# First keys loaded in two halves around the queries, first scores asked after half the keys, first hashes in the AV banks

## Chip, cores, metric

One core of a Trainium2 chip. The metric is the device time of the whole program in microseconds (us). The span of a profile is a little under the time of the same run (765.1 us against 766.81 us for the kernel before). With one core there is no second die to compare with, so "fast" here only says that a run lies within 1.5% of the fastest run of its kernel.

## The reference, cut

Hash attention over 4 batches, 8 heads, 768 tokens, 64 dimensions. A query sees the keys that share its 6-bit hash. The result feeds a dense mixture of 8 experts, which is most of the time and is not touched.

```python
q_bits = (np.einsum('bhsd,dk->bhsk', q, proj) > 0)      # k_bits likewise
mask = q_bucket[:, :, :, None] == k_bucket[:, :, None, :]
scores = np.where(mask, scale * np.matmul(q, k.transpose(0, 1, 3, 2)), -1e9)
attn = np.exp(scores - scores.max(-1, keepdims=True))
out = np.matmul(attn / (attn.sum(-1, keepdims=True) + 1e-09), v)
# [cut] then the experts: out += P[:, e:e+1] * (np.maximum(x @ w1[e], 0) @ w2[e])
```

## The kernel before

Heads are worked in groups of four. The mask is part of the matmul: six hash bits and one constant row are appended to the 64 dimensions (`KR` is 71 rows), with the key bits scaled by `BIG`. For every group, keys and queries are loaded, turned (transposed) on VectorE (DVE), hashed on TensorE (PE) and cast to f16. PE then makes scores for 24 units (4 heads x 6 key tiles), ScalarE (ACT) exponentiates each, PE multiplies with the values. I count these units from 0 through all groups, so unit 6 is the first of head 1, unit 24 the first of the second group, unit 30 of that group's head 1.

The first group goes through `at_once`. The second group is prepared between the first group's units; the hash bits of its heads 1 to 3 go out to DRAM and come back to other partitions (`put_bits`, `get_bits`).

```python
def fetch(n, what, eng=nc.gpsimd):          # [cut] addresses
    for name, src in (("k", k), ("q", q)):
        if name in what:
            pin(eng.dma_start(out=t, in_=src[...]))            # 768 KB, 6144 B per partition
    if "v" in what:
        for m in range(M4):                                    # 4 transfers to 32 partitions each
            pin(eng.dma_start(out=t[R * m:R * (m + 1)], in_=vsrc[m]))

def at_once():                              # the first group
    for name in "kq":
        d["pr" + name] = sps.tile([P, 2, 512], F32, tag="s", name="pr0")   # a bank of the scores' pool
        turn_qk(name, 0)                                       # DVE, then a GpSimd cast
        place(name, 0, 0, nc.scalar.copy)                      # ACT cast of head 0
        hash_twice(name, 0)                                    # PE, 4 matmuls into 4 x 32 partitions
        turn_qk(name, 1)
        # [cut] more casts on ACT, hash_twice(name, 1), warm-up matmuls, stacks of heads 2 and 3
    # [cut] key bits for all heads, moved to head 0; query bits of head 0; query bits for all heads
    place("q", 1, 1, nc.vector.tensor_copy)
    move("k", 1)                                               # DVE bit copies of head 1
    move("q", 1)
    # [cut] stack("q", 3), get_bits, cast_v() on GpSimd

def prepare(n):                             # later groups, [cut] turns, hash, stacks
    put_bits()                                                 # SP: bits to DRAM
    for h in range(1 if n < 3 else 0, 2):
        get_bits("k", h); get_bits("q", h)                     # SP: and back
    # [cut] stacks and bits of heads 2 and 3
    if n == 1:
        fetch(2, "kq")                                         # GpSimd's queue: 1.5 MB
        load_w(0, 1, pin=True, half=0)                         # and expert weights

fetch(0, "kq", nc.sync)
fetch(0, "v", nc.sync)
fetch(1, "kq", nc.sync)
# [cut] offsets, warm_up(16), the first group, then the loop over the units
```

The softmax here doesn't subtract the row's maximum and nothing guards it: scores larger than these inputs give would overflow.

## Time and profile before

| | before |
|---|---|
| time, median of 3 runs | 766.77 us (766.58 to 767.16) |
| DVE starts to turn the queries | 8.94 us |
| first exponential, unit 6, unit 17 | 14.27, 18.90, 28.91 us |
| next group's four transposes start | 18.21 us |
| first PE turn of finished heads | 27.97 us |

The prediction below shows the page's header, the chain and the DVE timeline. This is the queue of SyncE (SP) of before in order of time (start, length of the issue, engine, line, operation, out<-in):

```profile
25.90 0.53 SPq L422 DMA_DIRECT2D ds<-bt  x1
...
33.40 0.27 SPq L425 DMA_DIRECT2D ks<-ds  x1
33.72 0.30 SPq L425 DMA_DIRECT2D qs<-ds  x1
```

The second group's bits leave for DRAM (`ds`) at 25.90 and can be read back only when that write has landed, at 33.40: 7.5 us for 96 KB.

### The profile page before, as it was taken

Reading aid. Unit: us, or ns where it says so; the run is one execution under the profiler, and the core shown is the slowest. Engines: PE = TensorE matmul, PEld = TensorE weight load, DVE = VectorE, ACT = ScalarE, POOL = GpSimd, SP = SyncE. Lnnn points to the kernel's source line nnn. Section 1 sums busy time; section 2 is a strip of 40 time slices with the busy share of each in tenths; the row PEclk is TensorE's granted clock in tenths of the full one; section 3 lists DMA queues with packets and bytes.
Section 4 is the critical chain, followed back from the end, with each engine's and each line's share of the span. In section 5 each row is a group of like instructions: output and inputs, shape, how many; then the busy total and the mean of one; then the engine's idle time right before and its main releaser. Section 6 shows DMA issues by size and latency. Waiting matters only on the chain.

```text
span 765.1 us, 16738 instructions
## 1 busy us (share of the span) xinstructions
PE 747.5 (98%) x6294; PEld 517.2 (68%) x6294; DVE 567.4 (74%) x1261; ACT 514.0 (67%) x1027; POOL 318.3 (42%) x327
## 2 busy tenths in 40 slices
PE   8999999999999999999999999999999999999997
PEld 3655566566654677777777777777777777777664
DVE  6787666667579777777777777777777777777774
ACT  6986786678655777766666666666666666666661
POOL 6766353449200433443344334433543344324222
PEclk9999999999999999999999999999999999999999
DMA  8779447841030464776477648754964496443335
GB/s 227 203 195 227 126 128 174 175 124 27 2 56 8 83 108 80 125 126 115 90 130 132 112 84 144 121 95 83 171 118 90 91 165 112 84 84 83 84 77 145
DMA packets 41569, 88.08 MB, mean 115 GB/s; under 512 B 7232, under 2 KB 21840, under 8 KB 41488
## 3 DMA queue, kind: packets, MB, share of 16 engines
q0 software_dynamic: 27168, 69.49, 46.9%
q1 hardware_dynamic: 13324, 16.48, 8.2%
q10 hardware_dynamic: 996, 1.05, 0.6%
q8 instruction: 49, 0.80, 0.5%
q14 instruction: 32, 0.26, 0.1%
HBM read 53.05 MB, written 7.08 MB: 79 GB/s over the span
## 4 chain that ended last, share of the span: by engine, by line
PE 84%; DVE 6%; ACT 6%; issue 1%; DMA 1%; SPq 0%; ACTq 0%; DVEq 0%
PE a L829 18%; PE a L250 18%; PE d L829 13%; PE y L250 9%; PE st L570 6%; PE d L250 4%; ACT pt L573 4%; PE hp L647 4%; PE yp L662 3%; PE num L586 3%; PE pr L406 1%; PE hp L325 1%; PE yp L309 1%; ACT acc L241 1%; DVE hT L838 1%
## 5 line engine op out<-in xcount | busy, mean ns | idle before, releaser
L838 DVE CUSTOM_DVE_ANT_0 hT<-d,u 128x384 f16<-128x384 f32 x336 | 185.5, 553 | 96.2 <-ACT u L834 94.7
L254 ACT ACTIVATE vt<-a,p 128x256 f32<-128x256 f32 x324 | 153.3, 473 | 148.7 <-PE a L250 148.3
L834 ACT COPY u<-a 128x384 f32<-128x384 f32 x336 | 160.8, 479 | 23.5 <-PE a L829 19.9
L573 ACT ACTIVATE pt<-st 128x768 f16<-128x768 f32 x192 | 147.1, 809 | 42.5 <-PE st L570 41.8
L289 POOL DMA_DIRECT2D acc<-vt x72 | 62.0, 861 | 267.1 <-ACT vt L254 114.0
L250 PEld LDWEIGHTS <-hT 128*128 128x128 f16 x1296 | 126.3, 97 | 50.4 <-DVE hT L838 0.9
L250 PE MATMUL a<-t,hs 128*128 128x256 f16 x972 | 145.8, 273 | 2.2 <-ACT vt L254 1.0
L250 PEld LDWEIGHTS <-hs 128*128 128x128 f16 x972 | 94.8, 98 | 38.5 <-issue 2.8
L829 PEld LDWEIGHTS <-t 128*128 128x128 f16 x896 | 87.7, 98 | 36.4 <-issue 0.6
L829 PE MATMUL d<-xd,t 128*128 128x384 f16 x448 | 109.4, 326 | 0.3 <-DVE hT L838 0.3
L829 PE MATMUL a<-xT,s 128*128 128x384 f16 x448 | 109.4, 326 | 0.2
L570 PE MATMUL st<-qs,ks 71*128 71x384 f16 x384 | 94.0, 325 | 3.6 <-ACT pt L573 2.4
L250 PE MATMUL y<-t,hT 128*128 128x256 f16 x648 | 97.1, 272 | 0.0
L258 DVE SCALAR_TENSOR_TENSOR acc<-y,p,acc 128x256 f32<-128x256 f32 x162 | 77.4, 478 | 11.4 <-PE y L250 11.4
L134 POOL TENSOR_TENSOR t<-t 128x1024 f16<-128x1024 f16 (+1 forms) x39 | 81.9, 2108 | 0.1
L586 PEld LDWEIGHTS <-pt 128*128 128x128 f16 x1152 | 60.5, 97 | 25.9 <-ACT pt L573 0.4
L829 PEld LDWEIGHTS <-s 128*128 128x128 f16 x672 | 65.5, 98 | 17.5 <-issue 2.5
L586 PE MATMUL num<-va,pt 128*128 128x65 f16 x1152 | 66.5, 193 | 0.3 <-ACT pt L573 0.3
L868 ACT ACTIVATE hT<-a 128x384 f16<-128x384 f32 x112 | 54.0, 482 | 1.8 <-PE a L829 1.7
L829 PE MATMUL a<-xd,s 128*128 128x384 f16 x224 | 54.3, 323 | 0.8 <-ACT u L834 0.8
L829 PE MATMUL d<-xT,t 128*128 128x384 f16 x224 | 54.7, 326 | 0.0
L829 PE MATMUL a<-xT,t 128*128 128x384 f16 x224 | 54.7, 326 | 0.0
(121 smaller groups left out, 948.7 us busy)
## 6 DMA issues: line engine op xcount, KB each, us to landing
acc<-vt POOLq DMA_DIRECT2D x72, 512.0 KB, 4.8
t<-in_moe_w_dram POOLq DMA_DIRECT2D x26, 512.0 KB, 8.5
v<-in_v_dram POOLq DMA_DIRECT2D x28, 192.0 KB, 5.7
out_dram<-acc SPq DMA_DIRECT2D x78, 64.0 KB
acc<-in_k_dram POOLq DMA_DIRECT2D x6, 768.0 KB, 7.1
acc<-in_q_dram POOLq DMA_DIRECT2D x6, 768.0 KB, 12.2
t<-in_moe_w_dram POOLq DMA_DIRECT2D x3, 1024.0 KB, 12.0
ks<-t SPq DMA_DIRECT2D x60, 48.0 KB
```

Of the source, the lines that this page charges most:

```text
L134: pin(nc.gpsimd.tensor_tensor(o[:, sl], x[:, sl], y[:, sl], op=op))
L250: pin(nc.tensor.matmul(dst, hq[hn][:, fo, :], wq[wn][:, fo, :], start=first and fo == 0, stop=fo == FH - 1, skip_group_check=True))
L254: pin(nc.scalar.activation(out=vt[:, k], in_=a, func=Act.Copy, scale=p))
L258: pin(nc.vector.scalar_tensor_tensor(out=dst, in0=src, scalar=p, in1=dst, op0=Alu.mult, op1=Alu.add))
L289: pin(nc.gpsimd.dma_start(out=acc[:, b, i], in_=vt, accum_op=Alu.add))
L570: pin(nc.tensor.matmul(st[:, i, 0:HT], d["k"][0:KR, h, kt * P:(kt + 1) * P], d["q"][0:KR, h, i * HT:(i + 1) * HT], start=True, stop=True))
L573: pin(nc.scalar.activation(out=pt, in_=st[:, :, 0:HT], func=Act.Exp, scale=scale))
L586: pin(nc.tensor.matmul(num[:, j * (D + 1):(j + 1) * (D + 1)], pf[:, j * P:(j + 1) * P], va[:, h, kt, :], start=(kt == 0 and j == 0), stop= ...
L829: pin(nc.tensor.matmul(bk, wq[wn][:, do, f * P:(f + 1) * P], xq[xn][:, do, :], start=first and do == 0, stop=do == 1, skip_group_check=True))
L834: pin(nc.scalar.copy(t, bk))
L838: pin(add(TENSOR_ADD_SAT, out=dst, in0=bk, in1=u, s0=3e38, s1=0.0))
L868: pin(nc.scalar.activation(out=hT[:, f, hi], in_=a, func=Act.Relu))
```

## The change

The intent is to start on the queries sooner: load half the keys, then the queries, then the other half; hash and turn in that order; ask the first scores after half the keys. Hashes move to banks of the pool in which PE sums weights times values (the AV pool), so that they do not hold the banks of the first scores.

```diff
-    fetch(0, "kq", nc.sync)
+    fetch(0, {"k": (0,)}, nc.sync)          # 384 KB, 4 pieces of 768 B per partition
+    fetch(0, "q", nc.sync)
+    fetch(0, {"k": (1,)}, nc.sync)
 [cut]
-    nc.vector.memset(pb1, 0.0)
-    nc.vector.tensor_copy(pb1[R:2 * R, :, 0:NB], proj4[R:2 * R])
+    pin(nc.vector.memset(pb1, 0.0))
+    pin(nc.vector.tensor_copy(pb1[R:2 * R, :, 0:NB], proj4[R:2 * R]))
 [cut]
-    warm_up(16)
+    warm_up(13)
 [cut] in at_once:
-                d["pr" + name] = sps.tile([P, 2, 512], F32, tag="s", name="pr0")
 [cut] turns, casts and hashes by name
+                d["pr" + name] = avs.tile([P, 1, 512], F32, tag="n", name="pr0")
+            for c in range(2):
+                turn_keys(c, 0)             # half the keys: DVE, ACT cast, PE
+                place("k", 0, c, nc.scalar.copy, halves[0])
+                hash_twice("k", c, (0,))
+            [cut] casts of head 1
+            warm_up(3)
+            for c in range(2):
+                turn_qk("q", c)
+                place("q", 0, c, nc.scalar.copy)
+                hash_twice("q", c)
+                warm_up(2)
+            first_bits(0)                   # 2 DVE operations: head 0's key bits from PSUM
+            turn_keys(0, 1)
+            [cut] casts; hash_twice("k", 0, (1,)); warm_up(4); query bits of head 0
+            yield                           # the first scores are asked here
+            turn_keys(1, 1)
+            [cut] cast, hash_twice("k", 1, (1,)), stacks, query bits for all heads
+            first_bits(1)
+            [cut] key bits for all heads
+            place("q", 1, 0, nc.vector.tensor_copy)     # was on ACT
             place("q", 1, 1, nc.vector.tensor_copy)
+            move("q", 1)
             move("k", 1)
-            move("q", 1)
+            place("k", 1, 1, nc.vector.tensor_copy, halves[1])   # was on ACT
```

More of the change, by code (lines that the diff above doesn't have):

```diff
@@ L354, with key_half @@
     nat, grp = {}, {}
+    def key_half(t, x):
+        return t.rearrange("p (m t) d -> p m t d", m=M4)[:, :, x * KT // 2:(x + 1) * KT // 2, :]
     def fetch(n, what, eng=nc.gpsimd):
@@ L361, in fetch @@
                 t = acc_flat[:, x * DD:(x + 3) * DD].rearrange("p (m d) -> p m d", d=D)
+                nat[name, n] = t
+                if name == "k" and n == 0:
+                    for x in what["k"]:
+                        pin(eng.dma_start(out=key_half(t, x), in_=key_half(
+                            src[b, g * HG:(g + 1) * HG].rearrange("h (r m) d -> (h r) m d", r=R), x)))
+                    continue
                 pin(eng.dma_start(out=t, in_=src[b, g * HG:(g + 1) * HG].rearrange("h (r m) d -> (h r) m d", r=R)))
-                nat[name, n] = t
         if "v" in what:
@@ L443, in cast_v, with place, hash_twice, turn_keys @@
                 pin(nc.gpsimd.tensor_tensor(vs[:, hs, 0:D], v32[:, :, 0], v32[:, :, 2], op=Alu.add))
-        def place(name, h, c, copy):
-            pin(copy(d[name][32 * c:32 * (c + 1), h, :], trs[name][32 * h:32 * (h + 1), c, :]))
+        def place(name, h, c, copy, sl=slice(0, S)):
+            pin(copy(d[name][32 * c:32 * (c + 1), h, sl], trs[name][32 * h:32 * (h + 1), c, sl]))
         def at_once():
             bt = wk.tile([P, 2, S], F16, tag="t16", name="bt0")
-            def hash_twice(name, c):
+            halves = [slice(x * HT, (x + 1) * HT) for x in range(2)]
+            def hash_twice(name, c, xs=(0, 1)):
                 for g, table in enumerate((pb.rearrange("p c a r -> p c (a r)"), pb1)):
-                    for x in range(2):
+                    for x in xs:
                         o = 64 * g + 32 * x
                         pin(nc.tensor.matmul(d["pr" + name][o:o + 32, 0, 0:HT], table[:, c, :],
-                                             trs[name][:, c, x * HT:(x + 1) * HT], start=(c == 0), stop=(c == 1)))
+                                             trs[name][:, c, halves[x]], start=(c == 0), stop=(c == 1)))
+            def turn_keys(c, x):
+                pin(nc.vector.transpose(
+                    trs["k"][:, c, halves[x]].rearrange("p (t m r) -> p m t r", t=KT // 2, m=M4),
+                    key_half(nat["k", n], x)[:, :, :, 32 * c:32 * (c + 1)]))
+            def first_bits(x):
+                sl, to = slice(32 * x, 32 * x + NB + 1), d["k"][D:KR, 0, halves[x]]
+                pin(nc.vector.tensor_scalar(to, d["prk"][sl, 0, 0:HT], 0.0, 0.5, op0=Alu.is_gt, op1=Alu.subtract))
+                pin(nc.vector.tensor_scalar(to, to, BIG, None, op0=Alu.mult))
             def move(name, h):
@@ L469, in at_once @@
             for name in "kq":
-                d["pr" + name] = sps.tile([P, 2, 512], F32, tag="s", name="pr0")
-                turn_qk(name, 0)
-                place(name, 0, 0, nc.scalar.copy)
-                hash_twice(name, 0)
-                turn_qk(name, 1)
-                place(name, 0, 1, nc.scalar.copy)
-                if name == "k":
-                    place("k", 1, 0, nc.scalar.copy)
-                else:
-                    place("k", 1, 1, nc.scalar.copy)
-                    place("q", 1, 0, nc.scalar.copy)
@@ L481, in at_once @@
-                hash_twice(name, 1)
-                warm_up(9 if name == "q" else 4)
-                for h in range(2, HG if name == "k" else 3):
-                    stack(name, h)
+                d["pr" + name] = avs.tile([P, 1, 512], F32, tag="n", name="pr0")
[4 more added lines that the diff above has]
+            for c in range(2):
+                place("k", 1, c, nc.scalar.copy, halves[0])
@@ new lines, in at_once @@
+            warm_up(3)
+            for c in range(2):
+                turn_qk("q", c)
[4 more added lines that the diff above has]
+            turn_keys(0, 1)
+            place("k", 0, 0, nc.scalar.copy, halves[1])
+            place("k", 1, 0, nc.scalar.copy, halves[1])
+            hash_twice("k", 0, (1,))
+            warm_up(4)
+            for x in range(2):
+                sl = slice(32 * x, 32 * x + NB + 1)
+                pin(nc.vector.tensor_scalar(d["q"][D:KR, 0, halves[x]], d["prq"][sl, 0, 0:HT], 0.0, qoff[sl, 0:1],
+                                            op0=Alu.is_gt, op1=Alu.subtract))
@@ L485, in at_once @@
+            yield
+            turn_keys(1, 1)
+            place("k", 0, 1, nc.scalar.copy, halves[1])
+            hash_twice("k", 1, (1,))
+            for c in range(2):
+                pin(nc.gpsimd.tensor_copy(t16s["k"][:, c, :], trs["k"][:, c, :]))
+            stack("q", 2)
+            stack("k", 2)
+            stack("k", 3)
             k_, q_ = bt[:, 0, 0:HT], bt[:, 1, 0:HT]
+            pin(nc.vector.tensor_scalar(q_, d["prq"][:, 0, 0:HT], 0.0, qoff[:, 0:1], op0=Alu.is_gt, op1=Alu.subtract))
@@ L486, in at_once @@
+            first_bits(1)
             pin(nc.vector.tensor_scalar(k_, d["prk"][:, 0, 0:HT], 0.0, 0.5, op0=Alu.is_gt, op1=Alu.subtract))
             pin(nc.vector.tensor_scalar(k_, k_, BIG, None, op0=Alu.mult))
-            move("k", 0)
+            put("q")
             put("k")
-            for x in range(2):
-                sl = slice(32 * x, 32 * x + NB + 1)
-                pin(nc.vector.tensor_scalar(d["q"][D:KR, 0, x * HT:(x + 1) * HT], d["prq"][sl, 0, 0:HT], 0.0, qoff[sl, 0:1],
-                                            op0=Alu.is_gt, op1=Alu.subtract))
@@ L494, in at_once @@
-            pin(nc.vector.tensor_scalar(q_, d["prq"][:, 0, 0:HT], 0.0, qoff[:, 0:1], op0=Alu.is_gt, op1=Alu.subtract))
-            put("q")
+            place("q", 1, 0, nc.vector.tensor_copy)
             place("q", 1, 1, nc.vector.tensor_copy)
+            move("q", 1)
             move("k", 1)
-            move("q", 1)
+            place("k", 1, 1, nc.vector.tensor_copy, halves[1])
             stack("q", 3)
@@ L505, in prepare @@
         if n == 0:
-            at_once()
+            yield from at_once()
             return
@@ L694, in warm_up @@
             pin(nc.tensor.matmul(warm, tiny, tiny.unsqueeze(1).to_broadcast([P, 4, P]), start=True, stop=True))
-    warm_up(16)
-    for _ in prepare(0):
-        pass
+    warm_up(13)
+    opening = prepare(0)
+    next(opening)
     units = [(n, h, kt) for n in range(len(groups)) for h in range(HG) for kt in range(KT)]
@@ L705 @@
     pts = {0: scores(*units[0])}
+    drain(opening)
     left = 0
```

## The prediction

The forecast's sum came to T = 8.94 - 0.96 + 0.3 - 0.7 = about 7.5, 12.5 us of DVE in place of 9.27, and 766.77 - 1.4 + 3.2 = 768.6 us. Where it says that a copy is held by GpSimd, it means what before's trace shows: the four bit copies from 15.79 to 18.18 us took 0.42 to 0.88 us, and each ended 0.11 to 0.12 us after a GpSimd sum, where two with GpSimd idle took 0.25 each.

> **What bounds the kernel now.** I read the page's header and engine table first, then the chain that ended last, then each engine's instructions in order of time over the first 45 us, since the diff touches nothing after the first head group.
>
> ```profile
> span 765.1 us, 16738 instructions
> PE 747.5 (98%) x6294; PEld 517.2 (68%) x6294; DVE 567.4 (74%) x1261; ACT 514.0 (67%) x1027; POOL 318.3 (42%) x327
> ...
> PE 84%; DVE 6%; ACT 6%; issue 1%; DMA 1%; SPq 0%; ACTq 0%; DVEq 0%
> ```
>
> PE is busy 98% of the span, so on the page this is a PE kernel and DVE, at 74%, looks free. Only the opening can change, and there the averages mislead. The chain in order of time begins:
>
> ```profile
> 2.32 6.59 DMA acc<-in_q_dram
> 8.94 0.98 DVE acc L395
> 9.95 0.89 DVE acc L395
> ...
> 10.89 0.85 PE pr L455 x8
> 11.74 2.05 PE warm L694 x9
> 13.79 0.45 PE st L570 x2
> ```
>
> Columns are start, length, what. The queries' landing at 8.94 sets everything; the first scores come at 13.79. A little later the same chain runs through DVE again:
>
> ```profile
> 22.73 0.83 PE pr L406 x8
> 23.58 0.56 DVE bt L414
> ...
> 27.36 0.57 DVE xn L607
> 27.93 0.05 issue
> 27.97 0.51 PE xp L613 x6
> ```
>
> and the DVE timeline (start, length, then idle before it in brackets, if any) shows why:
>
> ```profile
> 8.94 0.98 DVE L395 STREAM_TRANSPOSE acc<-acc 128x768 f32<-128x768 f32 x1 [0.79 <-DMA acc<-in_q_dram]
> ...
> 14.54 1.23 DVE L446 CAST qs<-acc 32x768 f16<-32x768 f32 x1
> 15.79 0.95 DVE L461 COPY ks<-bt 7x384 f16<-7x384 f16 x2
> 16.77 1.41 DVE L461 COPY qs<-bt 7x384 f16<-7x384 f16 x2
> 18.21 3.56 DVE L395 STREAM_TRANSPOSE acc<-acc 128x768 f32<-128x768 f32 x4
> ...
> 28.52 0.56 DVE L614 COPY xT<-xp 128x768 f16<-128x768 f16 x1 [0.60 <-PE xp L613]
> ```
>
> Between the brackets at 8.94 and at 28.52 there is none: **DVE never idles from the queries' landing until 27.9 us**, and at 27.97 PE waits for it. So the opening is bound by DVE's queue, not by the first scores. Whatever DVE has to do between the queries' landing and 27.9 us counts in full.
>
> [...] the 32x768 cast starts at 14.54, as does a 0.83 us GpSimd sum, and ends at 15.77, 0.40 after that sum; the 7x384 bit copies take 0.25 us each at 12.04, while GpSimd is idle, but 0.42 to 0.88 us beside its sums at 15.8 to 18.2. [...] the halves are cut in 768 B pieces. No transfer in this trace has that size, so the cost of the cut is an estimate.
>
> **The change, part by part.** Let T be the moment DVE starts to turn the queries (8.94 before).
>
> *Loads.* The trace moves 409 GB/s from 4.0 to 6.3 us, so 768 KB takes 1.92 us. With half the keys ahead of the queries they end 0.96 earlier. Against that four times the pieces per byte: I allow 0.3. For it, the values' narrow rows (218 GB/s from 9 to 12.5 us) no longer follow directly on the queries, whose landing came 2.64 us after the keys' instead of 1.92: I give back 0.7. T = 8.94 - 0.96 + 0.3 - 0.7 = about 7.5 (7.1 to 8.2): **gain 1.4 us**.
>
> *DVE from T to the next group's transposes.* Before it is 18.21 - 8.94 = 9.27 us. After, in the program's order, with rows from this trace:
> - two query turns 1.84, to T+1.84;
> - first bits of half the keys from PSUM 0.61 and times BIG 0.26, the latter held by a GpSimd cast: T+2.84;
> - half a key turn, 0.5: T+3.4; query bits 2 x 0.61: T+4.65; second half turn 0.5: T+5.15; query bits for all heads 0.62: T+5.8;
> - the second half's bits wait for their hash. PE does that only after the first scores: hash 0.78 after T+3.4, four warm-ups 0.86, scores 0.33, hash 0.85, so T+6.3; bits 0.61 + 0.26: T+7.2; all heads' key bits 0.55 + 0.26: T+7.9 to 8.1;
> - seven copies where four bit copies and one cast stood: two casts, four bit copies, half a cast. GpSimd's value casts, 2 x 0.80 behind the last key cast at T+6.1, now end near T+7.8, and its six sums (0.83, 0.46, 0.46, twice) then run against these copies. Step by step, one copy per GpSimd instruction as from 14.5 to 18.2 before, they end at T+12.5.
>
> So 12.5 in place of 9.27, **3.2 us more DVE work behind the queries**. Its parts: half the key turns now come after T (1.0), the bits done twice for head 0 instead of copied (1.74 - 0.53), the extra cast and half cast (1.7), the wait for the second hash (0.5), less 0.45 for the four small offset instructions that now run before anything lands, and some 0.7 less elsewhere, mostly in moves that overlap a hold already counted. The transposes begin at 7.5 + 12.5 = 20.0 instead of 18.2.
>
> *First scores.* First exp at T+5.6 = 13.1 (14.27 before); second, behind hash and three warm-ups, at T+7.35 = 14.85 (15.25 before). The scores no longer wait for a bank held by the hashes, but the keys' second half sits in its place: 1.2 us gained on the first, 0.4 on the next five.
>
> *Then DVE takes it back.* Head 1's first scores (unit 6) need the last query bit copy and the first key one, T+11.67 = 19.2; exp 19.7 against 18.90: 0.8 late. The next group's hash needs the third transpose: T+15.23 = 22.7 against PE's arrival at 21.26 before: exp of unit 10 1.5 late. Mean, normalization, bits and normalization of head 1 follow without a gap as before (21.70 to 27.92, 6.22 us): T+16.0+6.2 = 29.7. PE's turn of the first heads, at 27.97 before, comes at 29.8: **1.8 us late**. From there ACT sets the pace (exps back to back for 11 us) with nothing to catch up; no later step of the chain is a transfer, so the shift should last. Sum: 766.77 - 1.4 + 3.2 = 768.6.
>
> *Without effect:* hash banks taken from the AV pool: the first AV bank is needed only after T+5.8, when its reader is done. PE issues 29 warm-up matmuls instead of 34, all of them while it would wait anyway, except the four and three counted above.
>
> **The rivals.** A: the intended one. The first exp, 1.2 us earlier, carries through: 765.6. For it: the chain's first 14 us is DMA, turns and first scores. Against: DVE's gap-free run to 27.9. B: my sum, 768.6. C: DVE and GpSimd do not collide where I put them; [...] GpSimd is busy until 18.6 now and later then, so 1 us is more likely: 767.6. D: 768 B pieces run as slowly as the values' rows, 218 GB/s instead of 409: half the keys take 1.8 us, T = 8.3 and no gain from the load: 769.4. E: the value casts come later, as they now queue behind the later key casts; GpSimd's sums end at T+12.1 = 19.6 (18.60 before); the mean matmul comes after 20 anyway, so nothing more.
>
> **Range and chances.** B has most weight, C and D bracket it, and A keeps about one chance in seven, as the order of the new instructions looks tuned on a chip. I take 768.3 us, 8 in 10 between 766.2 and 769.7. Two per cent is 15 us, more than the whole opening: faster 0.004, within 0.992, slower 0.004.
>
> **What would show it.** Queries' turn at 7.1 to 8.2. First exp near 13.1, second 14.85. Unit 6's scores stand waiting for a DVE bit copy, a wait not there now. The next group's transposes start near 20.0; first PE turn near 29.8, still released by DVE's xn; then a constant distance to the end. I am wrong if the transposes start before 18.5, if PE's turn comes before 28, or if the distance at 30 us is gone at 100.

## The result and the profile after

| | before | after |
|---|---|---|
| time, median of 6 runs each | 766.67 us (766.42 to 767.16) | 769.37 us (768.62 to 770.58) |
| span of the profiled run | 765.1 us | 766.9 us |
| queries' turn starts | 8.94 | 7.62 |
| first exponential | 14.27 | 13.47 |
| transposes of the next group start | 18.21 | 20.41 |
| first PE turn | 27.97 | 29.82 |

The ratio is 1.0036 (95%: 1.0023 to 1.0049), inside the 2% that counts as the same, though the change is slower beyond doubt. A ratio is the mean time of one kernel's fast runs over the mean of the other's in the same rounds, so it is not quite the quotient of the medians. The profiled run of after, 768.62 us, is its fastest: its trace explains +1.8 us, not the median's +2.7.

The page's header, engine row and chain shares of after hardly differ from before's; at this scale nothing can be seen:

```profile
span 766.9 us, 16736 instructions
...
PE 748.5 (98%) x6289; PEld 516.9 (67%) x6289; DVE 568.1 (74%) x1267; ACT 513.8 (67%) x1029; POOL 318.7 (42%) x327
...
PE 84%; ACT 7%; DVE 6%; issue 1%; DMA 1%; SPq 0%; ACTq 0%; DVEq 0%
```

The DVE timeline of after, to set against the one of before in the prediction:

```profile
5.68 1.04 DVE L469 STREAM_TRANSPOSE acc<-acc 128x384 f32<-128x384 f32 x2 [1.11 <-DMA acc<-in_k_dram]
7.62 1.84 DVE L403 STREAM_TRANSPOSE acc<-acc 128x768 f32<-128x768 f32 x2 [0.91 <-DMA acc<-in_q_dram]
9.49 0.55 DVE L475 TENSOR_SCALAR ks<-pr 7x384 f16<-7x384 f32 x1
...
14.25 0.55 DVE L475 TENSOR_SCALAR ks<-pr 7x384 f16<-7x384 f32 x1 [0.63 <-PE pr L465]
...
16.43 1.44 DVE L454 CAST qs<-acc 32x768 f16<-32x768 f32 x2
17.88 1.32 DVE L481 COPY qs<-bt 7x384 f16<-7x384 f16 x2
19.23 0.78 DVE L481 COPY ks<-bt 7x384 f16<-7x384 f16 x2
20.03 0.35 DVE L454 CAST ks<-acc 32x384 f16<-32x384 f32 x1
20.41 3.56 DVE L403 STREAM_TRANSPOSE acc<-acc 128x768 f32<-128x768 f32 x4
```

Behind the queries' turn the only idle time is the 0.63 us in which DVE waits for the hash of the second half. The seven casts and copies from 16.43 to 20.38 stand where five stood. The transposes come 12.79 us after the queries' turn began, against 9.27 before: +3.52 of work, -1.32 of earlier landing, so 2.20 later. PE now waits in two places:

```profile
19.79 0.50 PE L605 MATMUL st<-qs,ks 71*128 71x384 f16 x2 [1.28 <-DVE ks L481]
...
29.82 0.51 PE L648 MATMUL xp<-ident,xn 128*128 128x128 f16 x6 [0.22 <-DVE xn L642]
```

The first wait is new: head 1's scores (unit 6) stand for 1.28 us until DVE has copied the last bits. The chain of after shows how the first scores' lead is lost. It goes from PE's second hash to DVE and then through DVE alone up to the first PE turn (steps of DVE are left out at the dots):

```profile
13.11 0.33 PE st L605 x2
13.43 0.79 PE pr L465 x4
14.25 0.56 DVE ks L475
...
20.41 3.56 DVE acc L403 x4
...
29.21 0.57 DVE xn L642
...
29.82 0.51 PE xp L648 x6
```

Exponentials against before: first 0.80 us earlier, units 1 to 5 0.07 later, unit 6 1.48 later, unit 10 1.89, unit 17 1.85, units 32 to 144 1.60, end 1.8. Nearly all of this arises in the opening 30 us.

### The profile page after: what moved, and what is told of

The parts are those of the page before. It is cut to its first block, busy times and chain, and to the rows that moved or that the text cites. A ratio compares the mean times of both kernels' runs of the same rounds, so it can differ in the third digit from the quotient of the medians.

```text
span 766.9 us, 16736 instructions
## 1 busy us (share of the span) xinstructions
PE 748.5 (98%) x6289; PEld 516.9 (67%) x6289; DVE 568.1 (74%) x1267; ACT 513.8 (67%) x1029; POOL 318.7 (42%) x327
## 4 chain that ended last, share of the span: by engine, by line
PE 84%; ACT 7%; DVE 6%; issue 1%; DMA 1%; SPq 0%; ACTq 0%; DVEq 0%
PE a L867 18%; PE a L250 18%; PE d L867 13%; PE y L250 9%; PE st L605 6%; PE d L250 4%; ACT pt L608 4%; PE hp L682 4%; PE yp L697 3%; PE num L621 3%; ACT acc L241 1%; PE hp L325 1%; PE yp L309 1%; PE pr L414 1%; PE yp L210 1%
```

## The experiments

Twelve kernels ran, all correct. "Over its before" is the difference of medians to the kernel before on the same chip in the same rounds. Shifts are starts of exponentials in the profiled run against the first profile of before.

| run | median, range (runs) | over its before | ratio (95%) |
|---|---|---|---|
| x1_early_offsets | 766.64, 766.03 to 767.15 (5) | +0.13 | 1.0001 (0.9989 to 1.0013) |
| x2_av_banks | 766.82, 766.47 to 767.16 (5) | +0.31 | 1.0005 (0.9992 to 1.0018) |
| x3_loads_alone | 769.41, 767.69 to 772.85 (6) | +2.90 | 1.0042 (1.0026 to 1.0059) |
| x4_casts_on_act | 770.09, 768.63 to 773.05 (6) | +3.58 | 1.0052 (1.0035 to 1.0070) |
| x7_warm16 | 769.91, 768.62 to 770.78 (5) | +2.95 | 1.0034 (1.0021 to 1.0047) |
| x8_loads_warm16 | 769.87, 768.81 to 774.99 (6) | +2.91 | 1.0045 (1.0022 to 1.0067) |
| x9_offsets_av | 767.01, 765.70 to 767.88 (5) | +0.05 | 0.9995 (0.9982 to 1.0008) |
| x10_before_warm13 | 766.84, 766.12 to 767.56 (5) | -0.12 | 0.9994 (0.9981 to 1.0007) |
| x11_values_held | 769.62, 769.33 to 771.65 (5) | +3.13 | 1.0045 (1.0033 to 1.0058) |
| x12_loads_values_held | 768.91, 768.81 to 769.19 (5) | +2.42 | 1.0033 (1.0019 to 1.0046) |
| x13_act_casts_held | 769.62, 769.05 to 772.43 (6) | +2.67 | 1.0037 (1.0022 to 1.0052) |
| x14_before_values_held | 768.56, 766.92 to 769.91 (6) | +1.61 | 1.0013 (1.0000 to 1.0026) |

### First call: the parts one by one

**x1_early_offsets**: before, with only the two `pin`s, which put the four small offset instructions ahead of the loads' landing.

```diff
-    nc.vector.memset(pb1, 0.0)
-    nc.vector.tensor_copy(pb1[R:2 * R, :, 0:NB], proj4[R:2 * R])
+    pin(nc.vector.memset(pb1, 0.0))
+    pin(nc.vector.tensor_copy(pb1[R:2 * R, :, 0:NB], proj4[R:2 * R]))
```

> The kernel before, with only the query-offset and table-fill instructions pinned, so that the four small offset instructions run on DVE before any key has landed, as they do in the changed kernel. Theory (DVE's queue from the queries' landing to 28 us is the bound): about 0.4 us less work behind the landing, so the next group's transposes start near 17.8 instead of 18.21, PE's first turn comes near 27.6 instead of 27.97, and the time is 0.3 to 0.4 us shorter (766.3). Rival (DVE is not the bound, the first scores are): the first exp comes 0.3 earlier too, so the time alone does not tell; the rival says the gain equals that of the first exp.

Measured: no gain in time (+0.13), though its one profile showed the first exponential 0.55 us and the end 0.8 us earlier. What that profile really showed came out only with the second call, below.

**x2_av_banks**: before, with only the banks changed.

```diff
-                d["pr" + name] = sps.tile([P, 2, 512], F32, tag="s", name="pr0")
+                d["pr" + name] = avs.tile([P, 1, 512], F32, tag="n", name="pr0")
```

> The kernel before, with only the hash banks taken from the pool of the AV sums. Theory: the second scores no longer wait for the reader of the hash bank, second exp up to 0.3 us earlier, but DVE's queue is unchanged: transposes at 18.2, first turn at 28.0, time within 0.2 us of before. Rival (a freed score bank is worth its wait): 0.3 us shorter.

Measured: the same time within 0.2%. The banks alone do not matter.

**x3_loads_alone**: before's bits, copies and banks, with the new load order, the new turning order, the early offsets and 13 warm-ups.

```diff
-    fetch(0, "kq", nc.sync)
+    fetch(0, {"k": (0,)}, nc.sync)
+    fetch(0, "q", nc.sync)
+    fetch(0, {"k": (1,)}, nc.sync)
 [cut] turning and hashing by halves as in the change;
       all bits, moves, banks and the casts' engines as in before
```

> The kernel before with the loads of the changed one (half the keys, queries, other half) and the turns in that order, but no first scores at half the keys: all keys are hashed, the bits of head 0 are made once and copied, the casts stay where before had them, hash banks from the score pool. Theory: DVE's work from the queries' landing is about 9.8 us, not 12.8 as in the changed kernel and 9.3 before, and the landing is at 7.6 instead of 8.9; so transposes at about 17.4, first turn at about 27.1, time 0.8 us under before (765.9). Rival 1 (the split loads themselves cost): transposes at 20 or time over before. Rival 2 (the early first scores carried a gain): slower than the changed kernel.

Measured: far from expected, +2.90 at the median, with runs from 767.69 to 772.85. The profile (of the fastest run) shows the queries' turn at 7.20, as hoped, and then DVE waiting for keys:

```profile
9.64 1.04 DVE L469 STREAM_TRANSPOSE acc<-acc 128x384 f32<-128x384 f32 x2 [0.61 <-DMA acc<-in_k_dram]
```

The second half's landing is on the path. I had counted it as hidden.

**x4_casts_on_act**: the changed kernel, with the query cast and the half key cast of head 1 back on ACT.

```diff
+            place("q", 1, 0, nc.scalar.copy)
 [cut]
+            place("k", 1, 1, nc.scalar.copy, halves[1])
 [cut]
-            place("q", 1, 0, nc.vector.tensor_copy)
-            place("k", 1, 1, nc.vector.tensor_copy, halves[1])
```

> The changed kernel with the cast of head 1's queries and the half cast of its keys back on ACT. Theory: DVE loses 0.7 to 1.1 us of work behind the landing, so the transposes start at 19.4 to 19.7 instead of 20.41, unit 6 waits less than 1.28 us, first turn at 28.8 to 29.1, time 0.7 to 1.1 us under the changed kernel, still over before. Rival (ACT, not DVE, holds the changed kernel back): 0.5 to 1.3 us slower than the changed kernel, as ACT gets 1.3 us more before its first exps.

Measured: the step through DVE is right, but smaller than it looks.

```profile
7.20 1.84 DVE L403 STREAM_TRANSPOSE acc<-acc 128x768 f32<-128x768 f32 x2 [0.87 <-DMA acc<-in_q_dram]
...
19.08 3.56 DVE L403 STREAM_TRANSPOSE acc<-acc 128x768 f32<-128x768 f32 x4
```

The transposes start 1.33 us earlier than in after. Of this 0.42 us is the earlier landing of the queries (7.20 against 7.62), and 0.91 us is work taken from DVE's queue. Unit 17 stands at +0.52 instead of +1.85. The gain does not reach the end: +0.90 at unit 32, +1.18 at unit 88, span 766.9 as in after, median 770.09 (0.7 to 1.1 us under after was expected). So DVE's queue sets the first 30 us, and something else eats what is won there. One part of it is in the traces: in x4, x9, x10 and x11 PE waits 0.47 us near 40 us for DVE's copy of turned heads, and units 24 to 32 take 7.3 to 7.4 us; in the others, x8 apart, they take 6.7 to 7.0.

### Second call: is it the warm-ups?

The kernels with 13 initial warm-ups (after, x3, x4) had the widest spread, so I suspected PE's clock.

**x7_warm16**, **x8_loads_warm16**, **x10_before_warm13**: one number changed in the changed kernel, in x3 and in before.

```diff
-    warm_up(13)
+    warm_up(16)
```

(x10: 16 to 13.) **x9_offsets_av**: before, with the edits of x1 and x2 together.

> The changed kernel with 16 warm-up matmuls ahead of the first hash instead of 13. So far the profiles show PE's step from 426 to 216 ns per warm-up matmul at 4.5 to 5.2 us in the changed kernel and the two made from it or with its loads, and at 6.6 to 6.8 in two others; 13 matmuls at 426 ns end at 6.6 us, 16 at 7.9. New theory (warm-up): where the step would fall after 6.6, 13 matmuls do not last until it, PE stays at half speed for longer, and that is why the timed executions of the three kernels with 13 spread over 2 to 5 us and have a median above their profiled one, while those with 16 spread over 1 us. It expects: spread of about 1 us, median 768.3 to 768.8 (the 1.6 to 1.9 us that the profile shows), so 0.6 to 1.1 under the changed kernel. Rival (the spread comes from the 768 B loads, whose landing varies): spread still 2 to 5 us, median 769 or more.

> The kernel with the split loads alone, again with 16 warm-up matmuls ahead of the first hash instead of 13; nothing else. Warm-up theory: the spread of 767.7 to 772.9 shrinks to about 1 us and the median falls from 769.4 to 766.8 to 767.6. Rival (loads): spread of 3 to 5 us and median about 769.

> The kernel before with both small parts that cost nothing: offset instructions early and hash banks from the AV pool. DVE theory: transposes at 17.7 as with the early offsets alone, first turn at 27.5; profile 0.5 to 0.8 us under before; median 0.3 to 0.7 under before, near the edge of what five rounds can tell. This is the version that should beat both, if only just. Rival: no gain beyond 0.2 us.

> The kernel before with 13 warm-up matmuls ahead of the first hash instead of 16, nothing else. Warm-up theory: executions in which the step comes early (before 6.6 us) are as before, 766.0 to 767.1; the others lose 1 to 5 us; so median 767 to 769, spread 2 to 5 us. Rival (loads cause the spread): as before, 766.5, spread 1 us.

Measured: the warm-up theory falls. Sixteen warm-ups bring nothing back (+2.95 and +2.91), thirteen cost before nothing (-0.12). x9 shows no gain either (+0.05), so early offsets and AV banks are worth nothing that five rounds can see. In this call the spread belongs to the kernels with split loads (of before's own eleven runs, ten lie within 1.2 us and one is at 769.34); in the fourth call before's runs spread over 2.7 us too. DVE waits for keys in both traces of split loads of this call, x8 first:

```profile
11.00 1.04 DVE L469 STREAM_TRANSPOSE acc<-acc 128x384 f32<-128x384 f32 x2 [1.57 <-DMA acc<-in_k_dram]
```

```profile
11.28 0.58 DVE L469 STREAM_TRANSPOSE acc<-acc 128x384 f32<-128x384 f32 x1 [0.83 <-DMA acc<-in_k_dram]
```

The second line is of x7. Each load completes in sixteen parts, and the trace has the time of each. Of the last load that DVE needs (the queries in kernels of before's kind, the second key half in the others), the first and last part landed at:

| kernels of before's kind | first, last | first exponential against before |
|---|---|---|
| x1 | 7.69, 8.49 | -0.55 |
| x2 | 7.61, 8.69 | -0.22 |
| before | 7.63, 8.91 | 0 |
| x9 | 7.57, 9.02 | -0.07 |
| x10 | 7.63, 9.34 | +0.43 |

| split loads | first, last |
|---|---|
| after | 8.08, 9.56 |
| x3 | 8.02, 9.62 |
| x4 | 7.99, 9.88 |
| x8 | 8.11, 10.97 |
| x7 | 8.12, 11.26 |

Two things follow. The first table explains most of x1's "gain": its queries happened to land 0.42 us earlier. A difference of half a microsecond between two single profiles is landing luck here. In the second table the last part lands 1.5 to 3.1 us after the first. DVE reaches the second half at 10.49 in after, so up to there a late landing is hidden, and beyond it is paid.

What slows the last parts? The values come next in the same queue, to 32 partitions at a time; their 1536 B pieces took 65 ns each where the first few began (7 to 8 us in after) and 156 ns a microsecond later. From 9 to 10.5 us in before, where hardly anything but pieces of 1536 B ran, 220 GB/s were moved, against 409 from 4.0 to 6.3 us. In x7 the key pieces left over at 9 to 10 us took 96 ns instead of 36. So the values' transfers may hold up the last parts of the keys. That can be tried.

x7's own trace shows a second loss. These are windows of x7 and then of after (window, length, busy us and instructions of PE, PEld, DVE, ACT, POOL, granted PE clock, DMA share, GB/s):

```profile
17.00:21.00 4.00, 2.51 (x36) 1.80 (x34) 3.90 (x6) 2.69 (x4) 3.59 (x6) 0.98 0.38 77
21.00:24.00 3.00, 3.00 (x28) 2.24 (x27) 2.96 (x5) 1.62 (x2) 1.43 (x2) 0.50 0.24 60
```

```profile
17.00:21.00 4.00, 2.72 (x44) 2.00 (x42) 3.85 (x8) 2.69 (x4) 2.38 (x4) 1.00 0.40 81
21.00:24.00 3.00, 3.00 (x40) 1.69 (x37) 3.00 (x5) 2.34 (x4) 2.48 (x3) 1.00 0.13 31
```

In x7 the granted clock is 0.5 from 20.88 to 24.29, a window of 3.41 us, and 28 PE instructions fill the 3 us where after has 40. It follows on PE's wait for unit 6, 1.49 us long here. Against after, x7 is 0.62 us late at unit 1 (the landing), 0.83 where PE starts on unit 6, just ahead of the slow window, and 1.91 at unit 17, so the slow window cost about 1.1 us. PE was idle for 1.49 of the 3.41 us ahead of the slow window. After's wait at the same place, 1.28 us, was followed by no such window.

### Third call: hold the values

**x11_values_held** (the changed kernel) and **x12_loads_values_held** (x3): a 16-byte transfer that reads the queries makes the queue wait for their landing before it asks for the values (issued from 8.11 us on in x11 and from 7.88 in x12, against 3.59 in after).

```diff
+    held = scr.tile([1, 4], F32, tag="held", name="held")
+    pin(nc.sync.dma_start(out=held, in_=nat["q", 0][0:1, 0, 0:4]))
     fetch(0, "v", nc.sync)
-    fetch(1, "kq", nc.sync)
 [cut] in at_once:
             stack("q", 2)
+            fetch(1, "kq", nc.sync)
```

> The changed kernel with the four value loads of the first group held on the SP queue until the queries have landed (a 16-byte transfer that reads the queries goes ahead of them), and the second group's keys and queries asked after them. Why: in the five profiles so far of kernels with the split loads, the sixteen completions of the second key half end at 9.56, 9.62, 9.88, 10.97 and 11.26 us, up to 3 us after the first of them (8.0 to 8.1), while the value pieces that follow take 110 to 150 ns each; in x7 VectorE waited 0.83 us there. Theory L (the values' pieces slow the last engines of the second key half, the late landing puts the first scores and all behind them later, and this differs from run to run): the completions end at 9.2 us or before, VectorE waits for no key landing, and the time is 768.0 to 769.0 with a spread under 1.3 us; the values land about 1 us later, which may cost up to 0.5. Theory H (the spread is the TensorE clock's windows over the idle of the opening): time stays 769.4 to 770 and the spread near 2 us. If the completions stay ragged, the values are not what slows them.

> The kernel with the loads and the turning order alone (x3) and the same hold of the values. Theory L: the second key half lands by 9.2 us, so VectorE turns it right behind the queries with a wait of at most 0.2 us (0.61 and 1.57 in x3 and x8); the first exponential comes 0.3 to 0.6 us earlier than before; the time is 766.0 to 766.8, spread under 1.3 us. Theory H and any other theory that does not blame the landing: 769.0 to 769.9 as in x3 and x8, spread 2 us or more.

Measured: the mechanism is right, the size is not. The sixteen parts of the second half now land at 8.01 to 8.80 in x11 and 7.92 to 8.65 in x12, and DVE waits for no key in either. x12's five runs lie within 0.4 us, where x3 and x8 spread over 5 and 6. Four of x11's lie within 0.5, but the fifth is 771.65. The medians hardly fall: 769.62 and 768.91 where I expected 768 to 769 and 766.0 to 766.8.

For x12 the profile says why. DVE's lines:

```profile
9.35 0.99 DVE L469 STREAM_TRANSPOSE acc<-acc 128x384 f32<-128x384 f32 x2
10.86 1.23 DVE L515 TENSOR_SCALAR qs<-pr,qoff 7x384 f16<-7x384 f32 x2 [0.52 <-PE pr L465]
12.79 0.56 DVE L517 TENSOR_SCALAR bt<-pr 128x384 f16<-128x384 f32 x1 [0.70 <-PE pr L465]
```

With the keys in place, DVE waits for PE instead. Each half of the keys takes two hash steps of about 0.77 us (four PE instructions in 0.77 us in after; eight for all the queries in 0.78): a step with half the columns fills half the 32-partition outputs and took just as long. The second half's hash comes behind the queries' hash and two pairs of warm-ups, and the bits wait until 12.79; before had them at 11.16. The first exponential comes 0.67 us later than in before, where 0.3 to 0.6 earlier was expected, and unit 17 stands at +0.51, not below 0. Further on, x12 waits 0.44 us for bits from DRAM (below) and gets to the end at +2.1.

### Fourth call: DVE's step without the ragged landing, and the hold applied to before

**x13_act_casts_held**: x4 with x11's hold. **x14_before_values_held**: before, with its values held until DVE has turned the first half of the key dimensions.

```diff
                 turn_qk(name, 0)
+                if name == "k":
+                    held = scr.tile([1, 4], F32, tag="held", name="held")
+                    pin(nc.sync.dma_start(out=held, in_=trs["k"][0:1, 0, 0:4]))
+                    fetch(0, "v", nc.sync)
 [cut]
                     stack(name, h)
+                if name == "k":
+                    fetch(1, "kq", nc.sync)
```

> The kernel of x4 (the changed kernel with the query cast and the half key cast of head 1 back on ScalarE) with the values held as in x11: the step of VectorE's queue, measured without the ragged landing. If VectorE's queue behind the queries sets the end of the opening, as the prediction says: the next group's transposes start at 19.1 to 19.4 us (20.60 in x11, since 1.3 us of casts have left the queue), the first PE turn at 28.5 to 28.8 (30.01 in x11), and the time is 1.0 to 1.4 us nearer to its before than x11's +3.1, so +1.7 to +2.1, with a spread under 1.3 us. If the queue does not set the time and something later makes up for it: the same +3.1 as x11 in spite of the earlier transposes.

> The kernel before, with its first values held until VectorE has turned the first half of the dimensions of the keys, and the second group's loads asked after them. In the five profiles of kernels with before's loads the sixteen completions of the queries end at 8.49 to 9.34 us, and the first exponential follows them (8.49: -0.55 us, 8.69: -0.22, 9.02: -0.07, 9.34: +0.43 against 8.94). If the values' pieces slow the last of the queries too: the completions end at 8.3 to 8.6, the first exponential comes 0.3 to 0.6 us earlier and the time falls by 0.3 to 0.6 us, to a ratio of 0.9992 to 0.9996. Against it: the values land about 0.3 us later and the stacks of heads 2 and 3 are asked 0.8 us later, and if either is on the path, the time is equal or up to 0.5 us longer.

Measured, x13: the transposes start at 19.62 (20.60 in x11; 19.1 to 19.4 expected) and unit 17 stands at +1.06 (x11 +2.04). So 0.98 us arrives in full at 30 us: 0.83 taken from DVE's queue and 0.15 because the queries' turn starts at 7.66 instead of 7.81. The span falls by only 0.6, and the time over its before by 0.46, to +2.67 (+1.7 to +2.1 expected), with overlapping intervals: too little to call. Part of the difference is lost in the experts' phase, in small PE gaps whose size goes with the kernel. One of them, x13 and then x11:

```profile
734.83 0.28 PE L250 MATMUL d<-t,hT 128*128 128x256 f16 x1 [0.50 <-DVE hT L878]
```

```profile
735.18 0.28 PE L250 MATMUL d<-t,hT 128*128 128x256 f16 x1 [0.29 <-DVE hT L878]
```

x13 is 1.12 us behind before at unit 184 and 1.87 at this place; x11 is 2.23 and 2.22. Both kernels execute the same code there. At this place the gap is 0.50 to 0.52 us in x3, x4, x8, x12 and x13, 0.29 in after, x7 and x11, and nothing in before and the kernels of its kind. Behind unit 184 the first five lose 0.7 to 1.1 us more against before, the next three 0.1 to 0.6. What makes the gaps is open.

Measured, x14: the opening does what was expected. The queries land at 7.60 to 8.02, the first exponential comes 0.54 us earlier, and unit 32 still stands at -0.59. Then at unit 40 it is +2.66, and the time misses the forecast (+1.61 at the median, though the ratio's interval reaches down to 1.0000; the profiled run is the slowest of the six). The PE waits of x14 in that stretch, its SP queue, and its chain:

```profile
37.74 0.48 PE L576 MATMUL st<-qs,ks 71*128 71x384 f16 x2 [0.39 <-DMA qs<-ds]
...
45.56 0.48 PE L576 MATMUL st<-qs,ks 71*128 71x384 f16 x2 [1.97 <-DMA qs<-ds]
```

```profile
26.37 0.53 SPq L422 DMA_DIRECT2D ds<-bt  x1
...
35.10 0.27 SPq L425 DMA_DIRECT2D ks<-ds  x1
35.42 0.30 SPq L425 DMA_DIRECT2D qs<-ds  x1
```

```profile
26.37 8.71 DMA ds<-bt
...
38.84 6.63 DMA qs<-ds
```

The bits of the second group left for DRAM at 26.37 and could be read back at 35.10, after 8.73 us; head 1 (unit 30) stood waiting 0.39 us. The wait of 1.97 us, for head 2 (unit 36), has a further cause: its read, asked at 38.84, took 6.63 us to land. In x10 the bits came back even later (35.24) and head 2's read was asked later (38.88), but it landed after 2.34 us and PE waited for no bits. One difference is the read's place against GpSimd's request for the fourth group's keys: x10 asked its read 0.06 us after it, x14 1.34 us after it. In the 14 traces this read took 1.5 to 5.0 us where it was asked up to 0.06 us after that request, and 4.1 to 6.6 us where it was asked 1.2 us after it or later (x8, x12, x14). That the requested loads slow the read is argued, not shown.

The wait of 1.97 us then cost a second time: the clock record has 0.5 from 45.98 to 49.39. In the windows of x14 the mean clock shows it:

```profile
41.00:45.00 4.00, 2.33 (x30) 1.32 (x26) 3.15 (x8) 2.41 (x4) 2.12 (x4) 1.00 1.05 220
45.00:50.00 5.00, 4.44 (x32) 2.74 (x33) 2.44 (x6) 2.30 (x3) 0.41 (x1) 0.66 1.12 242
```

A like wait is in x8, 1.93 us at unit 30 for head 1's bits, which left for DRAM at 28.59 and could be read back only at 37.62. It takes x8 from +1.37 at unit 24 to +2.73 at unit 32:

```profile
41.06 0.48 PE L596 MATMUL st<-qs,ks 71*128 71x384 f16 x2 [1.93 <-DMA qs<-ds]
```

This wait brought no slow clock. In the clock record both slow windows begin a whole number of 3.413 us after the clock first rose (5 in x7, 12 in x14); the stretch at full clock in before and in after, 761.17 us in each, is 223 times that. On that raster x8's wait lies 1.32 us in one window and 0.61 in the next, while the 1.49 us of x7 and the 1.97 of x14 each lie in one. No threshold follows: near its end before has a window in which PE was idle for 1.76 us, and the clock was not halved behind it.

After has no such wait. Its bits could be read back sooner:

```profile
27.59 0.53 SPq L430 DMA_DIRECT2D ds<-bt  x1
...
31.97 0.27 SPq L433 DMA_DIRECT2D ks<-ds  x1
```

4.38 us instead of 8.73 in x14. With all 14 traces side by side, the time that this write takes goes with its place against GpSimd's request for the third group's keys:

| bits' write issued, against the request for the third group's keys | from write to read |
|---|---|
| after -0.38, x11 -0.38, x4 -0.32, x1 -0.06 | 4.38, 4.14, 5.87, 5.57 |
| x7 +0.01, x13 +0.05, before +0.07 | 3.93, 4.89, 7.50 |
| x9 +0.38, x2 +0.47, x10 +0.48, x3 +0.72 | 7.90, 8.09, 8.87, 7.96 |
| x14 +0.94, x12 +1.16, x8 +1.66 | 8.73, 8.36, 9.03 |

Issued up to 0.05 us after the request the write takes 3.9 to 5.9 us, issued 0.38 us after it or later 7.9 to 9.0. Before sits on the edge, with 7.50 at +0.07. That the 1.5 MB of loads and the expert weights delay the write is argued, as no run here took the loads away; the step of some 3 us is what is shown. Most of it is given back: head 1's read takes 4.8 to 5.2 us to land behind an early write and 1.5 to 2.9 behind a late one (3.3 in before), so that from the write's issue to the landing of these bits it is 9.3 to 11.0 us in the six traces with the early write and 10.7 to 12.2 in the other eight. PE waits for bits only where its slack is used up as well (x8, x12, x14; not before, x2, x3, x9, x10).

No version beats the kernel before. The best single run of the variants of before's kind is 765.70 (x9), 0.2 us under the lowest of before itself (765.92).

## Why the prediction was right, and where it was not

- **T, the queries' turn**: 7.5 predicted, 7.62 measured. The rival D (pieces as slow as the values) falls: a 768 B piece took 36 ns, a 6144 B one 234 ns, so a piece moved at 21.3 against 26.3 GB/s, and the allowance of 0.3 us for the cut was about right. The prediction could have read it: that no transfer of its trace had this size is a misreading, as the trace of before holds 1808 pieces of 768 B, median 36 ns, from 16.7 us on. Its 218 GB/s for the values' rows also counts 50 pieces of 6144 B that ran from 10.5 us on; before them it is 220.
- **DVE's work behind T**: 12.5 us predicted, 12.79 measured, so +3.5 in place of +3.2. The wait for the second hash, 0.5 in the sum, was 0.63. Two errors cancel: the steps ahead of the seven copies took 8.81 us (about 8.0 in the sum), and the copies 3.95 us (4.5 in the sum), 1.32 of it in two query bit copies of 0.79 and 0.53, where a copy took 0.25 with GpSimd idle (12.04 in before, 19.76 in after). The first three of the four bit copies ended 0.11 to 0.12 us after a GpSimd sum, as in before, but I tried no run without GpSimd's sums.
- **First scores**: 13.1 and 14.85 predicted, 13.47 and 15.32 measured: 0.4 to 0.5 late, so the first units gained less than claimed, and units 1 to 5 nothing. Rival A falls with it.
- **DVE takes it back**: unit 6's exponential 0.8 late predicted, 1.48 measured, with the predicted wait for the bit copy; unit 10 1.5 against 1.89; transposes 20.0 against 20.41; PE's turn 29.8 against 29.82. The last hit is in part luck: the transposes began 0.41 late, and from there to PE's turn it took 9.41 us, not the 9.76 of before that the sum kept. x4 and x13 confirm the step as a cause: their transposes start 1.33 and 0.98 us earlier, 0.91 and 0.83 of it taken out of DVE's queue, and unit 17 comes earlier by the same 1.33 and 0.98.
- **The lasting shift**: this is the weak step: "no later step of the chain is a transfer, so the shift should last". In the profiled run it nearly held: +1.85 at unit 17, +1.60 at unit 144, +1.8 at the end, 768.62 us where the sum was 768.6. Even there DVE's queue holds a transfer:

```profile
35.79 0.98 DVE L403 STREAM_TRANSPOSE acc<-acc 128x768 f32<-128x768 f32 x1 [1.91 <-DMA acc<-in_k_dram]
```

  But that run is the fastest of six, so that the sum comes within 0.1 us of it is luck; the median is +2.7. Three things that vary from run to run were missing from the sum, each seen in at least one trace: the landing of the second key half (0.83 us of DVE's wait in x7, 1.57 in x8), PE's clock dropping for 3.41 us after a wait (about 1.1 us in x7, and seen in x14), and the bits' way through DRAM (1.93 us of PE's waits in x8, 2.36 in x14). The new wait at unit 6 is the place where x7's clock fell (1.49 us there, 1.28 in after, where it did not fall), and the late second halves are those of the split loads (10.97 us in x8, 11.26 in x7). That any of them makes up the median is not shown.
- **What stays open**: what makes up the 0.9 us between after's profiled run and its median. No median run of after has a trace, but two things narrow it. One slow window takes 0.0022 off a run's mean granted clock (half of 3.41 us in 767); after's two middle runs, 769.35 and 769.38 us, have 0.999 and 1.000, so no such window is in them. And x11's profiled run is x11's median run, 769.62 us: its trace has none of the three, and it is still 2.8 us behind before, 2.04 of it at unit 17, 0.31 more by unit 32, 0.12 less by unit 184, 0.57 more behind it. So a median of that size needs none of the three. The runs of 771 to 775 us have no trace either, but their clocks are on record: 774.99 (x8) has 0.994, which is some 9 us at half clock (an estimate from 0.006 of 773 us; the idle end of a run counts in it: in after's profiled run, 0.999, the clock is 0.5 for the last 1.2 us), 772.85 (x3) and 772.43 (x13) have 0.996, and 772.57 (x4) has 1.000. So the clock has a part in some of them and not in all.

## What to carry to other kernels

Before moving a load forward, list what the engine behind it must still do until the next thing that waits for it: here DVE had no idle time for 19 us, so work put behind the queries counted nearly in full (2.20 us at the transposes, 1.85 at PE's turn), and the earlier first score counted nothing. When a change is worth a microsecond or two, look at each transfer on the way for its last part's landing and its slack, and at several profiles: single traces of the same opening differed by half a microsecond as the landings did (x10 against before: last part and first exponential both 0.43 us later). And where the sum from one trace and the median of the runs disagree, the missing term may be something that varies (a ragged landing, a close race between two queues, a clock window) or small shifts further on; the trace of a median run tells which, and here x11's showed none of the first kind.
